# Sparse attention and a maxout layer on one Trainium2 core: the values of three batches in groups of 768 queries instead of 512

## The chip, the cores and the metric

The kernel runs on one core of a Trainium2 chip. Time is device time in microseconds (us) of one execution of the whole kernel. The core has a matrix engine (TensorE, PE in the profile), two engines that read and write the matrix engine's output memory PSUM (VectorE, DVE in the profile; ScalarE, ACT), a general engine[...] (GpSimd, POOL), and SyncE (SP), which here issues every load and store.

## The reference

Queries, keys and values have 4 batches, 8 heads, 768 positions and 64 columns per head. Each query sees the keys within 15 positions of its own and, beside them, 24 block summaries: the maximum of the keys over each block of 32, with the mean of the values there. The attention's result is the input of a maxout layer.

```python
k_sum = k.reshape(B, H, nb, block, D).max(axis=3)          # block 32, nb 24
v_sum = v.reshape(B, H, nb, block, D).mean(axis=3)
scores_l = where(|i - j| < 16, scale * q @ k.T, -1e9)
scores_s = scale * q @ k_sum.T + log(block)
a = softmax(concat([scores_l, scores_s]))
x = a @ concat([v, v_sum])                                 # then (B * S, H * D) = (3072, 512)
h1, h2 = x @ w1, x @ w2                                    # (512, 1024) each
out = maximum(h1, h2) @ w_out                              # (1024, 512)
```

## The kernel before

**Maxout.** `maximum(h1, h2)` is computed as `h1 + relu(x (w2 - w1))`. So the kernel makes `wd = w2 - w1` (four quarters, line 607), the product `w1 w_out` once (`make_w1o`, lines 636 to 650, matmuls on line 644), and then for each of 12 groups of 256 rows (`maxout`, line 652): eight columns of hidden units by `x wd` (line 660, "hidden"), a relu out of PSUM, and the output rows as `x (w1 w_out)` (line 674) plus `relu(...) w_out` (line 681), copied out of PSUM and stored. For `make_w1o` the quarters of w1 are cast to bf16 (`w1b`) and turned on TensorE (line 618, "turn w1"). The product runs over the 1024 hidden units in two halves: the first needs the first half of w1 and of w_out, the second the other halves. w1, w2 and w_out are each loaded in two halves of 1 MiB.

**Attention.** Heads are taken in pairs, four pairs a batch. Keys and queries of a pair are loaded, cast to bf16 (`casts`, on POOL, ACT or DVE), turned on TensorE (line 434), and placed in SBUF (`kx`, `qx`) together with the block maxima (line 454). The queries of a head pair are cut in three groups of 256 (`NG = 3`); a head pair and a group make a unit, named (hp, grp). `scores` (line 501) takes two units at a time: their scores fill two PSUM banks, ScalarE takes the exponent of all 1024 columns (line 515), and a product with a mask (line 509) hides what a query must not see. In batch 0 the mask is added by matmuls instead. The results `pb` have six buffers. Values come with a column of ones, so that the sum of the weights comes out as column 65 of each product.

**Values.** `values` (lines 523 to 555) takes the two units of one `pb`: 16 matmuls of 65 columns into two PSUM banks, one bank for each unit; one reciprocal of the eight sums (line 549); one multiplication of 2 x 4 x 64 columns with them (line 552), which writes `xs`. In batches 1 to 3 the pairs of units are (hp, 0) with (hp, 1), and (hp-1, 2) with (hp, 2): six calls a batch. In batch 0 they are the two head pairs of one group, six calls as well. `turn_x` (line 575) turns the rows of `xs` for the maxout layer, in batches 1 to 3 all three groups of two head pairs at once.

**PSUM** has eight banks. Scores, values and turns take two neighbouring ones, a hidden or output product one.

**What sets the order.** Nothing is decided when the kernel is built: the string `ORDER` lists every operation with its engine (P, A, D, G for POOL, S for SP), its number in the order of creation, and the buffer slots that it takes. `Plan.run` issues them in that order, so each engine has a fixed queue, SP's loads, stores and copies among them. An engine waits at the first operation of its queue whose inputs or slots are not free. In the text, "load v00" is the first half of batch 0's values, "load k01" the keys of batch 0, head pair 1, "hidden 001" the second quarter of batch 0, group 0.

The head of the kernel before on SP: eight k and q loads of batch 0, v00, v01, the first halves of w1 and w2, the first half of w_out, the second half of w1, of w_out and of w2; then batch 1. On TensorE: all turns of k and q of batch 0, the scores and values in between, then two hidden products (line 660), and then the run of `w1 w_out` products (line 644).

Of the kernel before, what the change touches and what calls it, by code (L numbers as in the profile page):

```python
# [12 lines left out]
F32 = mybir.dt.float32  # L13
BF16 = mybir.dt.bfloat16
AX = mybir.AxisListType
ALU = mybir.AluOpType
# [4 lines left out]
    "G5:0 D6:0 D1 D2 D0 S40:0,0 S36:1,0 S12:2,0 S39:3,0 G23:0,0,0 G4:0 S13:0 S37:0 A101:0 S38:0 G7 "  # L21
    "G32:0,0 P103:0,0 G8 S41:0 A105:1,0 G68:1 A77:2 S14:4 D106:0 G9 P70:2,0 G93:3 P79:4,0 S16:5 A72:2,0 "
    "D81:0,0 G10 P95:6,0 A69:0 S42:6 D108 D82:1 A78:1 P71:0 S43:7 D73:0 A76:0 P80:0 D3 D92:2 A85:1 D102:3 "
    "P94:0 A100:2 D83 P104:0 D107 D75 D84 A96:3,0 D74 S62:2 P90:2 D97:0 P86:4 A91:0 D15:0,0 A109:3 D98 "
    "P24:6 D18 D99 D19 P114:2 S52:1 A25 D21 A87:1 P88:0 D20 G22 P110:6 A89:2 P112:4 D17:0 S65:3 D26 A28 "
    "P33:0 D29 D27 A34 A113:3 D30 P116:0 D35 S53:0 A31 P126:4 A111:4 G45:0 D117:0 D127:1 D118:0,0 A49:1 "
    "D128:0 G48:0 P121:6 P46:0 D122:2 S147:4,0 D123:1,0 P50:4 A47:1,0 D51:0 P119:6 A120:0 P124:0 P136:4 "
    "D125 G63:0 A115:5 P131:6 P460:0 S146:0 D44:0 A64:0 D137:0 A461:0 P458:1 D138:0 G55:0 P455:2 A459 "
    "S153:5,0 D59:1 P56:3 P60:0 D57:0 P452:5 A61:0 D132:1 D67:0 P449:3 A66:0 D11:0 S150:2,0 D133:0 P446:4 "
    "P450 S152:0 P453 D58:0 S149:6,0 P456 A219:0 D54:0 S151:0 P447 A457:0 D218:1 S148:0 P129:0 P134:6 "  # L30
    "P462:2 G163:1,0,0,0 D130:1 A135 D454:0 S156:7 A448:0 P464:0 D463 A258:2 S154:3 P141:6 P221:4,0 "
    "A451:0 P220:0 P480:1 D257:3 A465 S171:0,0 D142:2 A222:0,0 P478:2 G231:0 D481:1 S173:1,0 P476:3 "
    "D226:0 A479 G246:1 P471:0 D223:1 P260:1,0 D224 P139:4 P259:0 D245:2 P472 A140:2 D143:0 G230:3 "
    "A261:2,0 S170:0 P482:4 D225 D265:1 A477 P484:5 A483 D262:0 P144:6 G157:0,0 P227:1 P247:3,0 A145 "
    "P248:0 P485 D249:1,0 A228:1 P232:6,0 S175:4,0 D263 P233:0 P473 A234:3,0 D229 S172:0 A253:2 P500:1 "
    "D251 D264 D236 D235:1 G155:0 A474:0 P486 A501:2 P496:2 A487:1 D237 S162 D238:3 G295:2 P164:3 S161 "
    "P494:4 G307:1 A165 D250:0 A168 A497 P489:0 G294:3 D166 A495 D167 P242:5 D158 S169 P239:1 P266:3 "
    "A243:2 P498:7 D159 A267:4 P490 D252 D244 P502:5 A499 D160 S178:5 A240:0 S180:2 P269:3 P254:6 D268 "
    "S174:0 P503 S196:6,0 D306:0 A270:3 P491 D241 A255:5 G187:0,0,0,0 P284:1 D271 P504 D285:0 A492:2 "
    "D286:2,0 P507:3 A505:3 S493 D256 P275:6 P272:0 P278:4 D276:1 P508 D273:2 G179:0,0 D279:0 D274:0,0 "  # L40
    "P466:2 D280:0 S177:7,0 D277:0 P287:0 P281:4 P467 D282:2 S195:3,0 D288:0 D283:0 P509 G181:0 D289:0 "
    "S199:0,0 P296:6,0 P297:0 D510:4 P290:4 S176:0 A298:0,0 P292:0 G322:3 D291:3 P468 A302:0 S186 G321:2 "
    "D293 P188:3 P308:4,0 G183 S198:0 P309:0 P324:6,0 A310:3,0 P323:0 D314:3 P518:0 S185 A329:1 D311:1 "
    "P514:1 A519:1 S182 P536:4 A469:5 S200:1,0 G382:0 A515 P512:5 S197:0 A325:2,0 P520:0 G333:1 A190 "
    "S194:0 D326:0 A189 P516:2 G334:3 A513 D313 P335:6,0 P336:0 D517 P530:1 A337:1,0 D537:2 A341:2 P521 "
    "D328 S184 D312 D327 D299:1 A371:2 P315:4 P330:6 P534:2 S201:0 A316:4 D339 D338:0 P522 S506 D192 D535 "
    "P532:4 A523:2 S470 D531 A331:0 P552:5 D300 D340 D301 P525:2 G383:1 D553:0 P303:0 D191 G370:3 P345:6 "
    "S193 P526 A304:1 D317 S202:5 P543:5 S204:2 G211:1,0,0,0 D533 A346:2 S475 D332 P318:0 P342:3 P544 "
    "A319:3 D305 P527 A343:5 D320 S488 P545 D528:3 P548:6 D546:5 P550:7 D344 A549 P357:0 A551 P354:3 S529 "
    "P351:5 D358:1 P538:2 D352:2 D355:0 D353:1,0 P554:7 D356:0 P561:5 D359:0,0 A555 P360:3 D347 P384:6,0 "  # L50
    "S524 P373:0,0 D361:2 G410:0 P372:0 P385:0 D362:0 P562 A374:2,0 S547 G409:2 D390:1 A378:0 P556:3 "
    "G205:0,0 D386:0,0 P563 P348:0 A564:0 G203:0 P363:6 P539 D349:0 D364:1 S565 D365:0 P557 D350:0 S207 "
    "G209 P412:4,0 S208 P411:0 P368:6 P366:0 S206 A369:0 P558 S511 D367 P540 G210 D387:0 A417:3 P586:0 "
    "D375:1 A398:3 P572:1 A587:1 D376 D397:1 P590:6 A559:1 D541:3 A413:3,0 P602:7 D377 D591 P212:0 A603:0 "
    "P584:3 D214 A215 D414:1 A573:2 P568:2 A585 D388 D416 P604:4 D389 A213 A216 S217 P570:5 A605 A569 "
    "P379:6 D571 P399:0,0 P391:3 A380:0 P400:0 P579:2 D401:1,0 A392:3 P588:5 D403 D381 P566:6 D402:1 A589 "
    "P597:7 A567 D405:2 P592:3 D415 D404 P574:4 P394:5 P421:0 P580 A395:4 P593 A422:5 P575 D423 P406:5 "
    "P418:0 D396 P581 A407:1 D393 P594 A582:2 D408 A419:2 P608:5 P576 A609 D420 A595:5 P598 A577:0 S596 "
    "P439:0 P433:5 S560 P424:2 D440:2 P599 D434:1 S578 D425:0 D426:2,0 P606:4 A600:4 D441:0,0 P615:2 "
    "D435:0 S601 A607 P436:0 P427:5 P430:3 D437:0 P610:7 D438:0 D431:2 P616 D428:1 D432:0 P611 D429:0 "  # L60
    "P444:0 P442:3 A445:3 P617 D443 P612 A618:5 P674:5 P624:6 P644:3 D625:2 P658:4 P620:0 P628:1 A621 "
    "A659:1 P656:2 P642:6 D657 P622:0 D613:1 D645:0 P626:4 S614 A623 D643 S583 P640:2 A627 P638:7 P629 "
    "D639 P669:3 D641 P664:0 P633:6 P660:4 P634 D661 P662:7 P630 D663 P651:2 A631:0 P635 P646:4 D636:4 "
    "P665 S637 S542 P647 S619 P652 S632 P648 P666 A649:1 P653 S650 A667:2 P675 S668 D654:4 P670 P676 S655 "
    "P671 A677:3 A672:5 S678 S673 "
# [81 lines left out]
def kernel(  # L147
# [50 lines left out]
    xsr = Ring(tiles("xs", 3, [128, NG, 2, 4, D], BF16))  # L198
# [324 lines left out]
    def values(b, units, pb, prio):  # L523

        ps, tag = Buf(banks, "av", 2), f"{b}" + "".join(f" {hp}{grp}" for hp, grp in units)
        pair = units[0][0] // 2
        if (b, pair) not in xs:
            xs[b, pair] = Buf(xsr)
        x, inv, part = xs[b, pair], Buf(invr), Buf(Ring([None]))
        for _, grp in units:  # L530
            x_part.setdefault((b, pair, grp), []).append(part)

        def av():
            return bank(ps, 1024).rearrange("p (c n) -> p c n", c=2)[:, :, 0:4 * (D + 1)].rearrange(
                "p c (j d) -> p c j d", j=4)

        def mm():
            for c, (hp, grp) in enumerate(units):
                for u in range(2):
                    for a in range(2):  # L540
                        for par in range(2):
                            at = 256 * c + 128 * u + 64 * par
                            nc.tensor.matmul(out=av()[64 * par:64 * par + 64, c, 2 * u + a, :],  # L543
                                             lhsT=pb.ap[:, a, at:at + 64],
                                             rhs=vx[b].ap[:, 4 * grp + 2 * u + par, 2 * hp + a, 0:D + 1],
                                             start=True, stop=True)

        op("PE", 0.235, mm, read=[pb, vx_part[b][pair]], touch=[vx[b]], write=[ps], prio=prio, label=f"values {tag}")
        op("DVE", 0.2, lambda: nc.vector.reciprocal(out=inv.ap[:], in_=av()[:, :, :, D:D + 1]),
           read=[ps], write=[inv], prio=prio, label=f"inv {tag}")  # L550
        (hp, grp), (_, g1) = units
        op("DVE", 0.69, lambda: nc.vector.tensor_tensor(  # L552
            out=x.ap[:, grp] if g1 == grp else x.ap[:, grp:g1 + 1, hp % 2], in0=av()[:, :, :, 0:D],
            in1=inv.ap[:].to_broadcast([128, 2, 4, D]), op=ALU.mult),
           read=[ps, inv], write=[x, part], prio=prio, label=f"x {tag}")
# [6 lines left out]
    def turn_x(b, pair, grps, prio):  # L562
# [7 lines left out]
        def mm():  # L570
            for n in range(4 * n_grp):
                for half in range(2):
# [3 lines left out]
                                        in_=x.ap[r, grps[n // 4], n // 2 % 2, i:i + 2].rearrange("p a d -> p (a d)"),  # L576
# [9 lines left out]
    invr = Ring(tiles("inv", 3, [128, 2, 4, 1], F32))  # L586
# [114 lines left out]
    def later_attention(b, base):  # L701
        pbs = []
        for hp in range(NP):
            prio = base + 20 * hp
            prep(b, hp, prio, {"DVE": 0.56, "POOL": 0.83}, {"ACT": 0.83, "POOL": 0.83})
            for units in ([(hp, 0), (hp, 1)], [(hp - 1, 2), (hp, 2)])[0:1 + hp % 2]:
                pbs.append((units, Buf(pbr)))
                scores(b, units, "DVE", pbs[-1][1], prio + 5)
        for units, pb in pbs:
            values(b, units, pb, base + 20 * units[-1][0] + 10)  # L710
# [3 lines left out]
    def first_attention():  # L714
# [8 lines left out]
        for grp in range(NG):  # L723
            for pair in range(2):
                prio = (20, 120, 220)[grp] + 2 * pair
                values(0, [(2 * pair, grp), (2 * pair + 1, grp)], pbs[pair, grp], prio)
# [55 lines left out]
```

## Time and profile before

| | us |
|---|---|
| median of 8 runs | 172.89 (172.4 to 173.75) |
| the profiled execution | 172.86 |
| its span in the trace | 171.1 |

The span runs from the first to the last instruction of the trace; 1.76 us of the execution lie around it. The largest groups of instructions, by line:

| line | what | instructions | busy us | mean ns |
|---|---|---|---|---|
| 660 | hidden products, 256 columns | 384 | 47.3 | 277 |
| 681 | relu times w_out | 200 | 46.4 | 371 |
| 674 | x times (w1 w_out) | 100 | 24.2 | 371 |
| 543 | values, 65 columns | 384 | 9.2 | 202 |
| 515 | exponents, ACT | 24 | 26.0 | 1113 |
| 549 | reciprocals, DVE | 24 | 4.4 | 198 |
| 552 | weighting of the values, DVE | 24 | 15.6 | 684 |

Matmuls overlap in the array, so a mean duration on TensorE is longer than the time from one to the next; what a group takes in a row is read from the chain of waits. "PEld" is the loading of the stationary operand, which runs beside the products. A line of the timeline gives start, duration, engine, source line, operation, output and input; in brackets stands how long the engine was idle before it and what ended that.

### The profile page before, as it was taken

The numbers are of one execution on the slowest core, as the hardware profiler recorded it, in microseconds if no ns is written. First come the engines' busy times: TensorE is split into PE (matmuls) and PEld (weight loads), VectorE is DVE, ScalarE is ACT, GpSimd is POOL, SyncE is SP. The second block draws the span as 40 slices with busy tenths as digits, with TensorE's granted clock in tenths as the row PEclk, the third lists the DMA queues.
The fourth block names the chain that finished last, engine by engine and source line by source line (L and its number), as shares of the span: only waits on it lengthen the run. The fifth ranks groups of instructions, "written<-read, shape, count | busy, mean of one in ns | idle before, by whom it ended". The sixth has DMA issues, their size and how long they took to land.

```text
span 171.1 us, 5208 instructions
## 1 busy us (share of the span) xinstructions
PE 152.3 (89%) x2256; PEld 98.9 (58%) x2256; DVE 106.1 (62%) x198; ACT 91.5 (53%) x128; POOL 42.5 (25%) x62
## 2 busy tenths in 40 slices
PE   0156866999999999997999999999999999999992
PEld 0034555655856755475765764787555658876451
DVE  1275998668788997867777696674543761443110
ACT  4488499646659695068658332778368231320121
POOL 7620135800355402496040029400000000000000
PEclk9999995699999999999999999999999999999999
DMA  5999899999999789999985995854000600030175
GB/s 181 300 341 220 208 399 385 387 379 371 295 211 299 238 168 220 314 384 231 280 256 101 238 287 205 186 122 83 8 0 15 234 4 0 4 123 0 49 258 184
DMA packets 43430, 34.92 MB, mean 204 GB/s; under 512 B 25968, under 2 KB 37392, under 8 KB 43408
## 3 DMA queue, kind: packets, MB, share of 16 engines
q1 hardware_dynamic: 43408, 34.61, 73.0%
q8 instruction: 17, 0.28, 0.7%
q14 instruction: 5, 0.04, 0.1%
HBM read 25.17 MB, written 6.29 MB: 184 GB/s over the span
## 4 chain that ended last, share of the span: by engine, by line
PE 83%; DMA 6%; ACT 4%; SPq 3%; issue 1%; DVE 1%; ACTq 0%
PE banks L660 26%; PE banks L681 25%; PE banks L674 12%; DMA land<-in_v_dram 6%; PE banks L543 4%; PE banks L501 4%; PE banks L644 4%; PE banks L434 3%; SPq L305 3%; ACT vx L410 2%; PE banks L575 2%; ACT pb L515 2%; PE banks L349 1%; PE banks L346 1%; PE banks L618 1%
## 5 line engine op out<-in xcount | busy, mean ns | idle before, releaser
L660 PE MATMUL banks<-xt,wd 128*128 128x256 bf16 x384 | 47.3, 277 | 0.9 <-issue 0.9
L681 PE MATMUL banks<-wo,g 128*128 128x512 bf16 (+1 forms) x200 | 46.4, 371 | 0.0
L660 PEld LDWEIGHTS <-wd 128*128 128x128 bf16 x384 | 37.4, 99 | 9.3 <-issue 1.1
L515 ACT ACTIVATE pb<-banks,bias 128x1024 bf16<-128x1024 f32 x24 | 26.0, 1113 | 6.4 <-PE banks L501 6.3
L681 PEld LDWEIGHTS <-g 128*128 128x128 bf16 x200 | 18.1, 98 | 17.2
L406 ACT ACTIVATE g<-banks 128x512 bf16<-128x512 f32 x30 | 17.6, 601 | 17.1 <-PE banks L660 17.0
L674 PE MATMUL banks<-w1o,xt 128*128 128x512 bf16 (+1 forms) x100 | 24.2, 371 | 0.0
L408 DVE TENSOR_SCALAR g<-banks 128x512 bf16<-128x512 f32 x18 | 12.1, 689 | 17.2 <-PE banks L660 16.4
L410 POOL CAST kqb<-land 128x768 bf16<-128x768 f32 x17 | 14.0, 835 | 31.0 <-PE banks L434 15.0
L410 ACT COPY o<-banks 128x512 f32<-128x512 f32 (+1 forms) x18 | 10.0, 564 | 20.4 <-PE banks L681 20.2
L434 PE MATMUL banks<-identity,kqb 64*128 64x64 bf16 x384 | 10.0, 202 | 10.4 <-ACT kqb L410 5.8
L454 DVE TENSOR_REDUCE ks<-kx 128x24 bf16<-128x768 bf16 x16 | 15.0, 945 | 6.2 <-ACT kx L410 6.2
L410 ACT COPY kx<-banks 128x768 bf16<-128x768 bf16 x12 | 9.7, 805 | 13.4 <-PE banks L434 13.4
L509 DVE TENSOR_TENSOR pb<-pb,mask 128x1024 bf16<-128x1024 bf16 x18 | 12.0, 687 | 6.6 <-ACT pb L515 6.6
L552 DVE TENSOR_TENSOR xs<-banks,inv 128x512 bf16<-128x512 f32 x24 | 15.6, 684 | 0.3
L434 PEld LDWEIGHTS <-kqb 64*128 64x128 bf16 x384 | 7.6, 102 | 13.5 <-ACT kqb L410 6.1
L674 PEld LDWEIGHTS <-xt 128*128 128x128 bf16 x100 | 9.5, 98 | 8.7
L410 POOL CAST vb<-land 128x1536 bf16<-128x1536 f32 x6 | 8.9, 1494 | 13.9 <-DVE pb L509 9.4
L543 PEld LDWEIGHTS <-pb 128*64 128x64 bf16 x384 | 7.8, 116 | 6.3 <-issue 4.2
L543 PE MATMUL banks<-vx,pb 128*64 128x65 bf16 x384 | 9.2, 202 | 2.5 <-ACT pb L515 1.8
L501 PEld LDWEIGHTS <-kx 64*128 64x128 bf16 x416 | 8.6, 103 | 4.6 <-issue 4.0
L410 ACT COPY xt<-banks 128x512 bf16<-128x512 bf16 (+1 forms) x6 | 5.2, 870 | 9.7 <-PE banks L575 9.7
(66 smaller groups left out, 146.3 us busy)
## 6 DMA issues: line engine op xcount, KB each, us to landing
land<-in_k_dram SPq DMA_DIRECT2D x16, 384.0 KB, 8.2
land<-in_q_dram SPq DMA_DIRECT2D x16, 384.0 KB, 7.6
land<-in_v_dram SPq DMA_DIRECT2D x8, 768.0 KB, 10.4
out_dram<-o SPq DMA_DIRECT2D x19, 256.0 KB, 2.6
land<-in_moe_w_dram SPq DMA_DIRECT2D x4, 1024.0 KB, 11.1
land<-in_moe_w_out_dram SPq DMA_DIRECT2D x2, 1024.0 KB, 12.9
vx<-vb SPq DMA_DIRECT2D x3, 396.0 KB, 6.5
vx<-vx SPq DMA_DIRECT2D x3, 363.0 KB, 4.1
```

The source lines that it names most:

```text
L406: nc.scalar.activation(out=o, in_=i, func=ACT.Relu)
L408: nc.vector.tensor_scalar_max(out=o, in0=i, scalar1=0.0)
L410: {"DVE": nc.vector.tensor_copy, "ACT": nc.scalar.copy, "POOL": nc.gpsimd.tensor_copy, "SP": nc.sync.dma_start}[e](out=o, in_=i)
L434: nc.tensor.transpose(out=bank(ps, 2048, BF16)[:, at:at + 64], in_=src.ap[r, j].rearrange("p h d -> p (h d)"), identity=identity[r, r])
L454: op("DVE", 0.95, lambda: nc.vector.tensor_reduce(out=ks.ap[:].rearrange("p (t s) -> p t s", s=2), in_=kt()[:, :, 0:64].rearrange("p t (s ...
L501: nc.tensor.matmul(**m)
L515: op("ACT", 1.13, lambda: nc.scalar.activation(out=pb.ap[:].rearrange("p a n -> p (a n)"), in_=bank(ps, 1024), func=ACT.Exp, bias=bias[:], ...
L543: nc.tensor.matmul(out=av()[64 * par:64 * par + 64, c, 2 * u + a, :], lhsT=pb.ap[:, a, at:at + 64], rhs=vx[b].ap[:, 4 * grp + 2 * u + par, ...
L552: op("DVE", 0.69, lambda: nc.vector.tensor_tensor(out=x.ap[:, grp] if g1 == grp else x.ap[:, grp:g1 + 1, hp % 2], in0=av()[:, :, :, 0:D], ...
L660: nc.tensor.matmul(out=bank(ps)[:, 256 * s:256 * s + 256], lhsT=wd[n].ap[:, c, 128 * s:128 * s + 128], rhs=x_rows(b, grp)[:, c, :], start= ...
L674: nc.tensor.matmul(out=bank(ps, hi - lo), lhsT=x_rows(b, grp)[:, c, sl], rhs=w1o[c].ap[:, lo:hi], start=(c == 0), stop=False)
L681: nc.tensor.matmul(out=bank(ps, hi - lo), lhsT=g.ap[:, f, sl], rhs=wo[f // 2].ap[:, f % 2, lo:hi], start=False, stop=(f == FC - 1))
```

## The change

In batches 1 to 3 `values` takes the three units of one head pair, (hp, 0), (hp, 1) and (hp, 2), which lie in two different `pb` buffers, the third one shared with the neighbouring head pair. Their 24 matmuls fill the same two PSUM banks, six products of 65 columns in each, and one reciprocal of 12 sums and one multiplication of 2 x 6 x 64 columns serve all three: four calls a batch instead of six. Batch 0 keeps two units a call. `xs` is laid out with the head pair ahead of the group, so that the multiplication writes 768 columns in a row, and `turn_x` reads it by the new addresses.

```diff
-    xsr = Ring(tiles("xs", 3, [128, NG, 2, 4, D], BF16))
+    xsr = Ring(tiles("xs", 3, [128, 2, 4 * NG, D], BF16))
...
-    def values(b, units, pb, prio):
+    def values(b, units, pbs, prio):
...
+        n_unit = len(units)
+        per = 2 * n_unit
...
-            return bank(ps, 1024).rearrange("p (c n) -> p c n", c=2)[:, :, 0:4 * (D + 1)].rearrange(
-                "p c (j d) -> p c j d", j=4)
+            return bank(ps, 1024).rearrange("p (c n) -> p c n", c=2)[:, :, 0:per * (D + 1)].rearrange(
+                "p c (j d) -> p c j d", j=per)
...
-            for c, (hp, grp) in enumerate(units):
+            for n, (hp, grp) in enumerate(units):
+                pb, c = pbs[n]
...
-                            at = 256 * c + 128 * u + 64 * par
-                            nc.tensor.matmul(out=av()[64 * par:64 * par + 64, c, 2 * u + a, :],
+                            at, j = 256 * c + 128 * u + 64 * par, 4 * n + 2 * u + a
+                            nc.tensor.matmul(out=av()[64 * par:64 * par + 64, j // per, j % per, :],
...
-        op("DVE", 0.69, lambda: nc.vector.tensor_tensor(
-            out=x.ap[:, grp] if g1 == grp else x.ap[:, grp:g1 + 1, hp % 2], in0=av()[:, :, :, 0:D],
-            in1=inv.ap[:].to_broadcast([128, 2, 4, D]), op=ALU.mult),
+        op("DVE", 0.13 + 0.275 * n_unit, lambda: nc.vector.tensor_tensor(
+            out=x.ap[:, :, 4 * grp:4 * grp + 4] if g1 == grp else x.ap[:, hp % 2].rearrange(
+                "p (c j) d -> p c j d", c=2), in0=av()[:, :, :, 0:D],
+            in1=inv_ap().to_broadcast([128, 2, per, D]), op=ALU.mult),
...
-        for units, pb in pbs:
-            values(b, units, pb, base + 20 * units[-1][0] + 10)
+        for hp in range(NP):
+            units = [(hp, grp) for grp in range(NG)]
+            values(b, units, [pb_of[unit] for unit in units], base + 20 * (hp | 1) + 10)
```

The list of operations is shorter by 18 (three for each call less), and `ORDER` is written anew from its first word to its last: every engine's queue differs, and some casts, copies and relus stand on another engine. The head of it on SP is now: k of head pairs 1, 0 and 3, v00, q of 0, 1 and 3, v01, k and q of head pair 2, then the first half of w1, the first half of w_out, the second half of w1, the second half of w_out, the first and the second half of w2; then batch 1. On TensorE the first hidden product stands behind all eight `w1 w_out` products of line 644:

```diff
-    "P24:6 D18 D99 D19 P114:2 S52:1 A25 D21 A87:1 P88:0 D20 G22 P110:6 A89:2 P112:4 D17:0 S65:3 D26 A28 "
-    "P33:0 D29 D27 A34 A113:3 D30 P116:0 D35 S53:0 A31 P126:4 A111:4 G45:0 D117:0 D127:1 D118:0,0 A49:1 "
...
+    "P80:0 D74 D20 A85:1 D26 A102:1 P88:6 S62:7 D108 D19 P86:2 A89:0 P90:0 S52:3 P104:0 A87:1 D17:0 S65:1 "
+    "A91:2 D109:2 P33:6 G92:2 D30 P126:2 A34 G29 P116:4 A93:3 D127:0 P136:0 S43:0 D128:0,0 P94:6,0 D137:1 "
...
```

## The prediction

> **What bounds the kernel now.** I read the page's shares first, then the chain of waits, then the windows of the first 36 us, the transfers of the first 45 us, and the timeline where these pointed. The shares and the chain:
>
> ```profile
> PE 152.3 (89%) x2256; PEld 98.9 (58%) x2256; DVE 106.1 (62%) x198; ACT 91.5 (53%) x128; POOL 42.5 (25%) x62
> PE 83%; DMA 6%; ACT 4%; SPq 3%; issue 1%; DVE 1%; ACTq 0%
> ```
>
> TensorE carries the end. The span is 171.1 us, so it idles 18.8 us. By the windows of 5 us it is busy 15.15 of the first 30 us, so 14.85 us of the idle lies there; the rest is one stall of 0.88 us at 78 us with no releaser, and about 3 us behind the last matmul (168.0). VectorE is busy 62% and nearly off the chain: work taken from it is worth nothing by itself. What can move the end is (1) when TensorE's unbroken stretch starts, (2) how long its work takes after that, (3) a new stall in it. For (2), the chain in order of time shows a fixed price:
>
> ```profile
> 62.69 0.62 PE banks L501 x36
> 63.31 1.83 PE banks L681 x8
> 65.14 0.38 PE banks L543 x16
> 65.52 0.97 PE banks L681 x4
> 66.48 0.86 PE banks L674 x4
> 67.35 0.89 PE banks L543 x48
> ```
>
> Four 512-column matmuls take 0.86 us in stream and 0.97 behind small packed matmuls; 16 value matmuls take 0.38 alone and 48 take 0.89, that is 0.25 per 16 plus 0.12 once. So each separate run of small matmuls between large ones costs 0.11 + 0.12 = 0.23 us, whatever is in it.
>
> For (1), the windows (columns: stretch, busy time by engine, granted clock, DMA share, GB/s) and the transfers of the first 45 us in slices of 1.125 us:
>
> ```profile
> 18.00:19.00 1.00, 1.00 (x6) 0.46 (x4) 0.97 (x3) 0.00 (x0) 0.54 (x1) 1.00 0.39 69
> 19.00:20.00 1.00, 1.00 (x27) 0.78 (x28) 0.97 (x3) 0.81 (x2) 0.00 (x0) 1.00 0.51 75
> 27.00:28.00 1.00, 1.00 (x40) 0.94 (x38) 0.92 (x3) 0.68 (x1) 1.00 (x1) 0.50 1.04 385
> 32.00:33.00 1.00, 1.00 (x7) 0.72 (x6) 0.30 (x2) 0.60 (x1) 0.23 (x2) 0.55 1.05 385
> ...
> GB/s 0 52 339 341 205 291 382 366 391 384 282 221 206 220 233 220 65 148 404 410 391 390 399 380 388 390 380 388 390 395 377 385 376 371 371 376 374 373 371 317
> ```
>
> Loads run without a break from 2 to 45 us, at 385 GB/s but for the two v loads (about 220), with one hole at 18 to 20 us where the last v load ends and the first weight load starts: 69 and 75 GB/s over 2 us are 144 KB, which v's rate of 220 moves in 0.65 us, so about 1.4 us stand unused. The granted clock is one half from 26 to 33 us. The timeline then says what the loads hold up:
>
> ```profile
> 23.16 1.30 POOL L410 CAST w1b<-land 128x1024 bf16<-128x1024 f32 x1 [4.62 <-DMA land<-in_moe_w_dram]
> 25.92 2.35 POOL L607 TENSOR_TENSOR wd<-land,land 128x1024 bf16<-128x1024 f32 x1 [1.46 <-DMA land<-in_moe_w_dram]
> 30.02 2.04 POOL L410 CAST wo<-land 128x1024 bf16<-128x1024 f32 x1 [1.75 <-DMA land<-in_moe_w_out_dram]
> 32.70 0.69 DVE L410 CAST w1b<-land 128x1024 bf16<-128x1024 f32 x1 [0.70 <-DMA land<-in_moe_w_dram]
> 38.10 2.36 DVE L607 TENSOR_TENSOR wd<-land,land 128x1024 bf16<-128x1024 f32 x2 [1.02 <-DMA land<-in_moe_w_dram]
> ```
>
> These waits date the six weight loads: the 1st is in at 23.1, the 2nd at 25.9, the 3rd at 30.0, the 4th at 32.7, the 6th at 38.1; the 5th (w_out's second half) before its cast at 35.6. TensorE is unbroken from 34.35 us, when it gets the weights of the 4th load.
>
> **What the Trainium skill says.** "TensorE: Matmul & The Clock Gate", Part 1: the clock is half at the start and after an idle window of about 3.4 us, full after a busy one, and the windows run on their own phase. The trace agrees: half from 26.1 to 32.9, twice 3.4 us, behind a window with few matmuls. Its record says 1.00 before the first change, but six 256-column matmuls took 1.46 us at 17.7 and 0.84 at 22.6, so the start was slow too. "DMA: Bandwidth & Descriptors", Specifications: under 512 B a transfer is off line rate; v's rows of 256 B are the ones seen at 220 GB/s. "PSUM — Partial Sum Buffer", Specifications: a bank holds 512 FP32 values, so 6 x 65 = 390 columns fit where 4 x 65 = 260 stood; no wait comes from the size.
>
> **The change part by part.** *Values.* Batches 1 to 3 go from 18 groups of 16 matmuls, 18 reciprocals and 18 weightings to 12 of 24, 12 and 12. The matmuls are the same 288. VectorE: six reciprocals of 0.198 us go, 1.2 us. A weighting of 512 took 0.684 and a PSUM copy of 128 columns 0.289, so 1.03 ns a column and 0.95 us for 768: 12 x 0.95 = 11.4 against 18 x 0.684 = 12.3. Together 2.1 us less VectorE, hidden behind TensorE: 0 on the path. A pair's values now wait for its third unit's exponent; in the new order all three stand several large groups ahead, so I charge nothing; were that cover gone, one exponent and mask is 1.11 + 0.69 us a time. Order of parts in xs and the turned rows' addresses: same counts, nothing.
>
> *Order.* All queues are rewritten, and this is what counts. On TensorE, runs of small matmuls behind the first hidden product fall from 29 to 22.
>
> *Head.* On SP, v00 is now 4th, v01 8th, and the six weight loads go w1a, w_out a, w1b, w_out b, w2a, w2b instead of w1a, w2a, w_out a, w1b, w_out b, w2b (a and b are halves). The ten k, q and v loads ahead of them are the same bytes, so I keep the six dates by position. Then:
> - w1a at 23.1; POOL's two casts of it, 1.35 each: 25.8. The turn of w1 0 at half clock (1.04, the row of before at 27.4): 26.9. Three scores with mask at the cadence of 0.85 seen at 20 to 22 us: 29.5. The first half of w_out is in between 25.9 (2nd place) and 28 (lag of the 3rd), its cast on POOL 2.04: 29.9 at worst. So the first product w1·w_out starts near 30.0.
> - Four such halves 3.5, two turns 0.9 and a switch 0.2: 34.6; two values 0.6: 35.2. The second halves need w_out b, in at 32.7, and two VectorE casts of 0.65: 34.0, in time. Four halves 3.5, values and two turns 0.5, three switches 0.4: the first hidden product at 39.6.
> - It needs w2a, now 5th: 35.4, and POOL's subtraction 2.35: 37.8. Slack 1.8. The last needs w2b at 38.1 and VectorE (subtraction 1.2, a relu 0.7, a cast 0.55, subtraction 1.2 in turn): 43, against 39.6 + 5 x 0.87 + 0.1 = 44. Slack 1.
>
> At 39.6 the kernel before stands in its w1·w_out run, which ends at 41.14. So at that moment the changed one is ahead by 1.54 of it, one values group (0.25) and three turns of x (0.36), and behind by two hidden products (2 x 0.87): 0.4 us. From there it has 22 packed runs against 28: 6 x 0.23 = 1.4. Sum 1.8 us.
>
> *Two corrections.* Holes behind v loads: before has one of 1.4 us; after has two, v00 to q and v01 to k. The only v-to-q edge in this trace, at 51 us, shows one second at 168 GB/s, so 0.55 us. Two of those are 1.1, 0.3 better; bounds 0 and 2 x 1.4, so from 1.4 better to 1.4 worse. Clock: TensorE is dense from 25.8, so the first whole dense window ends between 29.2 and 32.6 by the phase; what lies behind 30.0 runs the products at half speed and loses half of it, 0 to 1.3 us, 0.5 in the mean; 1.7 if one more gap spoils that window. Before lost nothing lasting, since the 4th load held it until 34.35.
>
> 172.86 - 1.8 - 0.3 + 0.5 = 171.3 us. The 172.86 is the profiled execution (span 171.1 and 1.76 around it); the median shown is 172.89, so the two frames agree. The tail is kept at 3 us: the last group still ends in two half copies and stores.
>
> *In the dense part.* One spot is tight: near 105 us the copy of an output on ScalarE needs a buffer that a store frees, and SP has that store behind the spread of the means, two k loads and two v loads. Before, from that spread's issue at 90.4 the v loads ended at about 100.8 and the next store by 102: some 11.5 us. Two k loads and one store more make 14.2, with the copy 15; my count of TensorE's groups between the means and the turn that needs the bank gives 17 to 18. Covered by 2 us; priced at 0 with an end of 2 for the range.
>
> **The rivals.**
> - *Forecast (0.55):* earlier products and fewer packed runs, 171.3; own range 169.9 to 172.3.
> - *More (0.10):* no holes and a full clock from 30 us: 172.86 - 1.8 - 1.4 = 169.7. For it: SP has the loads queued well ahead. Against it: the one v edge that I can see is not free.
> - *Even (0.14):* the clock stays half through the first products (1.7): 172.8. For it: the phase is free and the head has idle windows. Against it: turns and scores fill 25.8 to 30.
> - *Slower (0.21):* v is cut in two in the queue, and each cut leaves a hole like the one at 18 to 20 us. All weight loads are then 1.4 us late, the products start 1.4 later, and the late start leaves 1.7 at half clock: 172.86 - 1.8 + 1.4 + 1.7 = 174.2. It decides from 1.8 us of delay on. For it: TensorE has no other work in the new order, since both hidden products that bridged 30 to 33 us now stand behind the products with w_out.
> - That the change does not do what it says can be left out: the new order has 12 values groups for three batches.
>
> **The numbers.** About 0.3% (0.5 us) is what a measurement tells from no change. Forecast and more give faster but for a few hundredths: 0.63. Even, and the upper edge of the forecast: 0.15. Slower 0.22. The range takes the forecast's, most of "more" and the lower part of "slower", where one hole is 1.4 and the clock costs 1: 169.4 to 173.8.
>
> **What would show it.** Right: 18 weightings, 6 of 0.68 and 12 near 0.95 us; the first hidden product at 38.5 to 40.5; TensorE unbroken from about 30; chain pieces of 0.97 rarer. Wrong: w2a's subtraction later than 39 us; TensorE's end not earlier than 166.7 though the first hidden product came by 39.6 (then stalls in the dense part, to be looked for at 105 us); small runs that cost less than 0.23.

## The result, and the profile after

| | us | runs | ratio to before, 95% interval |
|---|---|---|---|
| before | 172.86 median (172.03 to 173.75) | 32 | |
| changed kernel | 170.62 median (168.26 to 172.18) | 11 | 0.983, 0.980 to 0.986 |
| changed kernel, measured again | 170.03 median (169.51 to 171.14) | 6 | 0.9816, 0.978 to 0.985 |

By the medians the kernel became faster by 2.2 to 2.9 us, by the ratios by 2.9 to 3.2; the prediction was 171.3, 1.6 us less than before. The medians are of all runs, the ratios here and below only of those within 1.5% of a kernel's fastest (six of the eleven in the first row of the changed kernel), and its first profiled execution, 171.99 us, lies above that band, so the lines below are from the second one: 171.14 us, span 169.4. That too is 1.1 us above its median, so the trace shows less of the gain than the runs do.

The page's shares and the chain of waits, where the page of before had 152.3 us of TensorE and 83% of the chain on it:

```profile
PE 150.2 (89%) x2256; PEld 97.4 (58%) x2256; DVE 108.8 (64%) x187; ACT 91.2 (54%) x125; POOL 41.7 (25%) x66
PE 64%; SPq 15%; DMA 7%; DVE 6%; issue 3%; ACT 2%; POOL 1%; DVEq 0%; ACTq 0%; POOLq 0%
```

TensorE's busy time fell by 2.1 us with the same 2256 matmuls (by 0.8 in the first profile). The chain now leaves TensorE twice in the dense part, by VectorE and by SP's queue with a store: two waits are new there, and both are taken up below. VectorE has eleven instructions less and yet 2.7 us more: two copies of 3.17 us stand on it that before didn't have there.

The values in the chain in order of time (start, length):

```profile
126.85 0.86 PE banks L681 x4
127.71 0.88 PE banks L546 x48
128.59 0.97 PE banks L688 x4
```

The weightings in the groups by form (busy time, mean ns, idle before):

```profile
L557 DVE TENSOR_TENSOR xs<-banks,inv 128x768 bf16<-128x768 f32 x12 | 11.1, 953 | 0.2
L557 DVE TENSOR_TENSOR xs<-banks,inv 128x512 bf16<-128x512 f32 x6 | 3.9, 684 | 0.1
```

Twelve weightings have 768 columns, and batch 0's six keep 512. 48 value matmuls are now two groups of three units and take the same 0.88 us as three groups of two did (0.89). The price at the edges is the same, 0.97 against 0.86.

The head, first in four windows of 1 us (engines' busy time, clock, DMA share, GB/s):

```profile
18.00:19.00 1.00, 0.92 (x6) 0.65 (x6) 0.99 (x2) 1.00 (x2) 0.73 (x1) 1.00 1.06 386
19.00:20.00 1.00, 1.00 (x35) 0.62 (x35) 0.58 (x2) 0.68 (x3) 0.94 (x2) 1.00 1.10 397
27.00:28.00 1.00, 1.00 (x23) 0.64 (x18) 0.99 (x2) 1.00 (x2) 0.00 (x0) 0.50 1.04 385
32.00:33.00 1.00, 1.00 (x22) 0.46 (x22) 0.84 (x2) 0.00 (x1) 0.00 (x0) 1.00 1.09 393
```

The transfers of the first 45 us, in slices of 1.125 us:

```profile
GB/s 0 29 253 381 360 284 230 226 306 370 361 263 218 225 303 373 378 400 382 386 382 386 395 379 391 382 391 390 382 388 377 377 373 371 378 359 284 246 207 116
```

And the timeline of the same stretch, with what waits for the weight loads:

```profile
22.99 2.10 POOL L409 CAST w1b<-land 128x1024 bf16<-128x1024 f32 x2 [1.70 <-DMA land<-in_moe_w_dram]
25.61 1.05 ACT L409 CAST wo<-land 128x1024 bf16<-128x1024 f32 x1
25.64 1.04 POOL L409 CAST wo<-land 128x1024 bf16<-128x1024 f32 x1 [0.54 <-DMA land<-in_moe_w_out_dram]
27.40 2.97 PE L651 MATMUL banks<-wo,vx 128*128 128x512 bf16 x8
28.35 1.29 DVE L409 CAST w1b<-land 128x1024 bf16<-128x1024 f32 x2 [0.20 <-DMA land<-in_moe_w_dram]
33.74 2.35 POOL L614 TENSOR_TENSOR wd<-land,land 128x1024 bf16<-128x1024 f32 x1 [7.07 <-DMA land<-in_moe_w_dram]
37.83 5.41 PE L667 MATMUL banks<-xt,wd 128*128 128x256 bf16 x48
```

The hole of before at 18 to 20 us (69 and 75 GB/s) is gone: 386 and 397, and neither of the two v loads of 220 GB/s leaves one behind it. The first half of w_out is cast as soon as it is in, its two quarters at once on POOL and ScalarE, so the first product with w_out starts at 27.4 instead of 33.4 us. Its eight matmuls take 2.97 us, since the clock is at first still half (0.50 in the window of 27 to 28 us). The first hidden product stands at 37.8 (38.6 in the first profile), and from there 48 hidden matmuls run in one piece.

In the dense part, three lines of the timeline of the first profiled execution:

```profile
60.56 3.17 DVE L409 COPY vx<-vx 32x5808 bf16<-32x5808 bf16 x1
68.33 1.02 PE L681 MATMUL banks<-w1o,xt 128*128 128x512 bf16 x4 [1.61 <-DVE g L407]
106.07 0.86 PE L581 MATMUL banks<-identity,xs 64*128 64x64 bf16 x47 [0.54 <-ACT o L409]
```

The timeline of the second at the same places:

```profile
62.95 1.89 DVE L508 TENSOR_TENSOR pb<-pb,mask 128x1024 bf16<-128x1024 bf16 x3
64.75 1.47 POOL L409 CAST vb<-land 128x1536 bf16<-128x1536 f32 x1 [8.12 <-DMA land<-in_v_dram]
65.49 1.28 DVE L508 TENSOR_TENSOR pb<-pb,mask 128x1024 bf16<-128x1024 bf16 x1
68.82 0.52 PE L581 MATMUL banks<-identity,xs 64*128 64x64 bf16 x23 [0.17 <-DVE xs L557]
70.51 0.20 PE L581 MATMUL banks<-identity,xs 64*128 64x64 bf16 x1 [1.17 <-issue]
105.23 0.86 PE L581 MATMUL banks<-identity,xs 64*128 64x64 bf16 x47 [0.54 <-ACT o L409]
```

From 59 to 71 us VectorE has hardly any free time (busy 11.7 of 12 us): the spread of batch 1's means (3.17 us in both executions, in before a DMA of SP), four masks, a relu, four weightings. Where masks fall beside a cast on POOL, one takes 1.28 us instead of 0.63, and TensorE waited 1.61 us for the relu behind them in the first execution, 0.17 us in the second. The wait at 105 us is the same in both: ScalarE's copy of an output needs a buffer that a store frees. The 1.17 us with no releaser is of the kind of the 0.88 us of before at 78 us; the first execution has none (see the end).

### The profile page after: what moved, and what is told of

Same layout as the page of the kernel before. It is cut to its first block, busy times and chain, and to the rows that moved or that the text cites. A ratio compares the mean times of both kernels' runs of the same rounds, so it can differ in the third digit from the quotient of the medians.

```text
span 170.3 us, 5181 instructions
## 1 busy us (share of the span) xinstructions
PE 151.5 (89%) x2256; PEld 98.6 (58%) x2256; DVE 110.0 (65%) x187; ACT 91.1 (54%) x125; POOL 42.9 (25%) x66
## 4 chain that ended last, share of the span: by engine, by line
PE 65%; SPq 15%; DMA 8%; DVE 5%; issue 2%; ACT 2%; POOL 1%; DVEq 0%; ACTq 0%; POOLq 0%
PE banks L667 22%; PE banks L688 19%; PE banks L681 9%; SPq L304 8%; PE banks L651 5%; DMA land<-in_moe_w_dram 5%; PE banks L500 4%; SPq L326 4%; SPq L699 3%; DMA out_dram<-o 3%; PE banks L433 2%; PE banks L546 2%; DVE vx L409 2%; DVE pb L508 2%; PE banks L581 2%
## 5 line engine op out<-in xcount | busy, mean ns | idle before, releaser
L667 PE MATMUL banks<-xt,wd 128*128 128x256 bf16 x384 | 45.7, 273 | 0.0
L409 POOL CAST kqb<-land 128x768 bf16<-128x768 f32 x21 | 19.2, 934 | 43.7 <-PE banks L433 21.1
L405 ACT ACTIVATE g<-banks 128x512 bf16<-128x512 f32 x34 | 20.0, 605 | 18.6 <-PE banks L667 15.2
L514 ACT ACTIVATE pb<-banks,bias 128x1024 bf16<-128x1024 f32 x24 | 25.6, 1113 | 5.8 <-PE banks L500 5.7
L409 ACT COPY o<-banks 128x512 f32<-128x512 f32 (+1 forms) x15 | 8.6, 570 | 19.8 <-PE banks L688 10.8
L508 DVE TENSOR_TENSOR pb<-pb,mask 128x1024 bf16<-128x1024 bf16 x18 | 13.9, 796 | 5.8 <-ACT pb L514 5.7
L407 DVE TENSOR_SCALAR g<-banks 128x512 bf16<-128x512 f32 x14 | 9.6, 687 | 11.3 <-PE banks L667 11.2
L409 ACT COPY xt<-banks 128x512 bf16<-128x512 bf16 (+1 forms) x7 | 6.6, 955 | 17.0 <-PE banks L581 13.1
L557 DVE TENSOR_TENSOR xs<-banks,inv 128x768 bf16<-128x768 f32 (+1 forms) x18 | 15.0, 862 | 0.3
L409 DVE COPY o<-banks 128x512 f32<-128x512 f32 (+1 forms) x10 | 6.6, 662 | 13.0 <-PE banks L688 13.0
L409 POOL CAST vb<-land 128x1536 bf16<-128x1536 f32 x6 | 8.8, 1467 | 11.7 <-PE banks L500 7.4
L500 PE MATMUL banks<-qx,kx 64*128 64x64 bf16 (+2 forms) x416 | 10.2, 199 | 0.9 <-ACT qx L409 0.9
```

Of the source, the lines that this page charges most:

```text
L405: nc.scalar.activation(out=o, in_=i, func=ACT.Relu)
L409: {"DVE": nc.vector.tensor_copy, "ACT": nc.scalar.copy, "POOL": nc.gpsimd.tensor_copy, "SP": nc.sync.dma_start}[e](out=o, in_=i)
L500: nc.tensor.matmul(**m)
L508: nc.vector.tensor_tensor(out=o, in0=o, in1=m, op=ALU.mult)
L514: op("ACT", 1.13, lambda: nc.scalar.activation(out=pb.ap[:].rearrange("p a n -> p (a n)"), in_=bank(ps, 1024), func=ACT.Exp, bias=bias[:], ...
L557: op("DVE", 0.13 + 0.275 * n_unit, lambda: nc.vector.tensor_tensor(out=x.ap[:, :, 4 * grp:4 * grp + 4] if g1 == grp else x.ap[:, hp % 2].r ...
```

## The experiments

"Before" in each is the kernel before, measured beside it on the same chip. Diffs of the order are given in the names of the operations.

**1. Only the wide values, in the order of before.** Each three-unit group stands where the later of its two-unit groups stood; 27 packed runs instead of 28.

```diff
-  PE: values 1 00 01 | ... | values 1 02 12        (18 groups in batches 1 to 3)
+  PE: values 1 00 01 02                             (12 groups)
```

> The three-unit values alone, in the order of the kernel before: each wide group stands where the later of its two narrow groups stood. Theory (the gain of the change is its new order: earlier products, fewer packed runs): VectorE does about 2 us less, but hidden behind TensorE; 27 packed runs behind the w1 w_out products against 28, so 0.2 us less; 172.3 to 173.3 us, with the kernel before at 172.9. Rival (the gain is the shorter VectorE work and the shared weighting): close to the changed kernel, 170.3 to 171.3 us.

Measured: 173.62 us, before 173.13; ratio 1.0034 (1.0015 to 1.0052). The order of the head is as before; the values alone gain nothing, and this is even a little slower. The code part of the change, taken by itself, isn't the gain.

**2. Only the new order, with the narrow values.**

```diff
-  PE: values 1 10 11 12 | values 1 00 01 02 | (2 large) | values 1 30 31 32 | values 1 20 21 22 | ...
+  PE: values 1 10 11    | values 1 00 01    | (2 large) | values 1 02 12 | values 1 30 31 | values 1 20 21 | ...
```

The third units of two head pairs follow as one group in the next run of small matmuls (`values 1 22 32` one run further on).

> The code of before (18 narrow values groups for batches 1 to 3) in the order of the changed kernel: each three-unit group is replaced by its two-unit group at its place, and the pair's third units follow as a narrow group in the next run of small matmuls, so that the packed runs are 23 as in the changed kernel; VectorE does 2.1 us more. Theory (the order alone gains, the wide values nothing): 170.3 to 171.3 where before stands at 173.0, ratio 0.985 to 0.990, not distinguishable from the changed kernel. Rival (the three-unit values are needed for the gain, by VectorE or by PSUM coming free sooner): 172.0 to 173.0, ratio 0.994 to 1.000.

Measured: 175.79 us, before 172.88; ratio 1.0147 (1.0099 to 1.0195). Both expectations missed: it is 5.8 us slower than the changed kernel measured beside it (170.03). Its timeline shows seven waits of TensorE for VectorE, 5.3 us together, where the changed kernel's second profile has 0.17 us and its first 1.61; four of them:

```profile
67.76 1.02 PE L672 MATMUL banks<-w1o,xt 128*128 128x512 bf16 x4 [1.23 <-DVE g L406]
103.95 0.44 PE L541 MATMUL banks<-vx,pb 128*64 128x65 bf16 x16 [0.77 <-DVE xs L550]
108.50 0.53 PE L432 MATMUL banks<-identity,kqb 64*128 64x64 bf16 x24 [1.03 <-DVE xs L550]
139.45 0.41 PE L573 MATMUL banks<-identity,xs 64*128 64x64 bf16 x16 [0.78 <-DVE xs L550]
```

The first is for a relu, at the place where the changed kernel's first profile waits too. In the other six, values and turns wait for a weighting (`xs`), which holds their banks or their rows. The new order leaves two large groups between values and their next user; with the third units a run later, that is too short. So the order, as it stands, needs the wide values, though they gain nothing without it. Other places for the third units weren't tried.

**3. The price of a packed run.** The changed kernel with ten more runs: a large group is moved between two small ones. The first of these places is at 93 us, most lie behind 100; one of them:

```diff
-  PE: turn q33 | turn k32 | hidden 221
+  PE: turn q33 | hidden 221 | turn k32
```

> The changed kernel with ten large groups of TensorE moved forward by one place, each from behind a pair of small groups to between the two, all behind 100 us: the same matmuls, ten more runs of small ones. Theory (each separate run costs 0.23 us): 2.3 us more, 172.5 to 173.5 against 170.6. Rival (the 0.97 against 0.86 in the chain is only how the ends of overlapping matmuls are modelled): 170.6 within 0.5.

Measured: 173.32 us, before 173.23; ratio 0.9983 (0.9957 to 1.001). Against the changed kernel's 170.62 that is 2.7 us for ten, 0.27 each, with intervals of about 0.5 us on either side. The traces are sharper: from the scores at 93 us, just ahead of the first moved group, to the last matmul TensorE takes 75.27 us here. In the changed kernel's second profile it is 73.57 with the 0.54 of waiting at 105 us, which this run doesn't have, and 72.91 in the profile of experiment 8 with the stores early, which hasn't either. That is 2.2 to 2.4 us for ten, the 0.23 each that was read from the chain; so these are no matter of how the ends of matmuls are modelled.

**4. The new load order undone.** The changed kernel with the first half of w2 loaded second, as in before.

```diff
-  SP: w1a, w_out a, w1b, w_out b, w2a, w2b
+  SP: w1a, w2a, w_out a, w1b, w_out b, w2b
```

> The changed kernel with w2's first half loaded second again, as before, so that the first half of w_out comes third and everything behind it one place later. Theory (the place of the loads sets when the products start): the first product starts 2 to 3 us later than its 28.2, and all behind it; 172.3 to 173.6 us against 170.6. Rival (TensorE has slack there, since it waits for the 5th load anyway): 170.6 within 0.5.

Measured: 174.06 us, before 173.13; ratio 1.0039 (1.0017 to 1.0062); 3.4 us slower than the changed kernel, more than expected. TensorE stands before the first products and before the turns of w1:

```profile
31.16 1.89 PE L649 MATMUL banks<-wo,vx 128*128 128x512 bf16 x7 [1.18 <-POOL wo L407]
34.02 0.41 PE L623 MATMUL banks<-identity,w1b 64*128 64x64 bf16 x16 [0.98 <-DVE w1b L407]
```

The first hidden product stands at 41.9 us. One megabyte earlier in SP's queue costs more than the whole change gains: in the new order nothing else is there for TensorE to do between 29 and 34 us.

**5. The new load order alone, in the kernel before.** The two early hidden products go behind the products with w_out.

```diff
-  SP: w1a, w2a, w_out a, w1b, w_out b, w2b
+  SP: w1a, w_out a, w1b, w_out b, w2a, w2b
-  PE: hidden 001 | hidden 000 | w1o (8 groups)
+  PE: w1o (8 groups) | hidden 001 | hidden 000
```

> The kernel before with nothing but its head changed: loads in the order w1a, w_out a, w1b, w_out b, w2a, w2b, and the two hidden products of 001 and 000, with their subtractions and relus, behind the w1 w_out products. Theory (the head is about half of the gain): the products start 3 to 5 us earlier than 34.35 in the trace, the first hidden product comes near 39, and the time falls by 0.5 to 1.5 us, to 171.4 to 172.4. Rival (the head is hidden by what follows, or the wide values are the gain): 172.9 within 0.3.

Measured: 174.17 us, before 173.13; ratio 1.0061 (1.0042 to 1.008). Missed: a loss instead of about 1 us gained.

```profile
31.00 1.01 PE L642 MATMUL banks<-wo,vx 128*128 128x512 bf16 x2 [0.32 <-ACT wo L408]
41.14 0.19 PE L573 MATMUL banks<-identity,xs 64*128 64x64 bf16 x1 [0.41 <-ACT g L404]
```

The load comes earlier, but the second quarter's cast stands on ScalarE behind exponents, and behind the early products nothing fills TensorE; when the hidden products come, the turns behind them wait for relus. In this form, without the casts and the filling work, the load order is worth nothing.

**6. The whole head of the changed kernel, in front of the order of before.** Every queue up to the first hidden product is the new one (39 groups on TensorE, 22 loads), with narrow values and 28 packed runs behind it.

```diff
-  PE: ... turn w1 0 | turn w1 1 | turn x000 | ... | hidden 001 | hidden 000 | w1o ...
+  PE: ... turn w1 0 | scores 0 20 30 | scores 0 21 31 | scores 0 22 32 | w1o ... | hidden 001 | hidden 000
```

> The kernel before with the changed kernel's whole head (all queues up to the last w1·w_out product, 39 groups on TensorE, with its load order and its casts), and the order of before behind it; narrow values, 28 packed runs behind the last w1·w_out product as before. Theory (the new head brings about 1.3 us when it is taken whole, the fewer packed runs the rest): 171.2 to 172.2 us where before stands at 173.0, ratio 0.990 to 0.996; first hidden product at 38.4 to 38.9. Rival (the head brings nothing, as the moved loads alone did, and the gain is all in the later order): 172.6 to 173.4, ratio 0.998 to 1.002.

Measured: 173.17 us, before 172.88; ratio 1.0026 (1.0003 to 1.0049). The first hidden product comes at 38.6 as expected, but the time is the rival's:

```profile
38.61 1.92 PE L658 MATMUL banks<-xt,wd 128*128 128x256 bf16 x16
42.91 1.03 PE L658 MATMUL banks<-xt,wd 128*128 128x256 bf16 x8 [1.03 <-ACT xt L408]
```

At 42.9 the join between the two orders loses 1.03 us: a hidden product waits for a copy of turned rows that ScalarE has behind two relus and two casts. So that one was moved:

```diff
-  ACT: relu 001 | relu 000 | cast q10 | w1o 3 | xt 011
+  ACT: xt 011 | relu 001 | relu 000 | cast q10 | w1o 3
```

> The kernel with the changed kernel's head and the order of before behind it, with one instruction moved: ScalarE's copy of the last turned x of the head stands ahead of the first relu instead of behind two relus and two casts, where its hidden product waited 1.03 us for it. Theory (the whole head is worth about 1.1 us, and the join to the old order had eaten it): 171.8 to 172.5 us where before stands at 173.0, ratio 0.993 to 0.998. Rival (the head brings nothing lasting; the next wait takes the place of this one): 172.8 to 173.5, ratio 0.999 to 1.003.

Measured: 173.52 us, before 173.16; ratio 1.0036 (1.0014 to 1.0057). Missed again, and the reason is in the trace:

```profile
27.84 1.90 PE L642 MATMUL banks<-wo,vx 128*128 128x512 bf16 x8
37.26 1.92 PE L658 MATMUL banks<-xt,wd 128*128 128x256 bf16 x16
43.80 0.83 ACT L408 CAST kqb<-land 128x768 bf16<-128x768 f32 x1 [1.82 <-POOL kqb L408]
45.17 1.91 PE L658 MATMUL banks<-xt,wd 128*128 128x256 bf16 x16 [2.12 <-ACT w1o L408]
```

The hidden products now start at 37.3, earlier than in any other profile, and the wait of 1.03 us is gone. In its place TensorE waits 2.12 us for a copy of `w1o` out of its bank. That copy stands on ScalarE behind the cast of q13, and q13 is the seventh of batch 1's loads in the new load order where it was the third in the old one. The cast starts at 43.8 us here and at 43.9 in the run before, however early TensorE is. The trace of the run before has ScalarE waiting 1.01 us for the load of q there, the one here for a cast of POOL; so it is the loads, or a cast behind them, that date it. The changed kernel has six hidden products in one piece at this place (48 matmuls, 37.83 to 43.2 us), just until batch 1's turns are ready. The start that the head gains is kept by what stands behind it. What the head alone is worth, free of a join, these runs don't tell.

**7. VectorE's time.** The changed kernel with the reciprocal and the weighting of three units cut in two, one for each bank.

```diff
-  inv: reciprocal 2 x 6          x: multiply 2 x 6 x 64
+  inv: 2 reciprocals of 6        x: 2 multiplications of 6 x 64
```

> The changed kernel with the wide reciprocal and the wide weighting of batches 1 to 3 cut in two, one for each PSUM bank: 12 more reciprocals of 0.2 us and 12 more weightings, 4.3 us more VectorE work in all. Theory (VectorE is off the path but for the stretch at 58 to 70 us): 170.5 to 171.6 us against 170.6. Rival (the sharing is what makes the kernel faster): 172.5 us or more.

Measured: 171.13 us, ratio 0.9879 (0.9847 to 0.9911); 0.5 us above the changed kernel by the medians, 0.8 to 1.1 by the ratios, whose intervals just overlap.

```profile
L564 DVE TENSOR_TENSOR xs<-banks,inv 128x384 bf16<-128x384 f32 x24 | 11.7, 541 | 0.0
L558 DVE RECIPROCAL inv<-banks 128x6 f32<-128x6 f32 x24 | 3.1, 171 | 2.9 <-PE banks L546 2.9
```

The two groups take 11.7 and 3.1 us here, 11.1 and 2.2 in the changed kernel's second profile. So VectorE has not 4.3 but 1.5 us more, since neighbouring instructions overlap: as much as the wide values save in experiment 1 (104.6 us busy against 106.1 in before). Taking that saving back costs at most 1.1 of the 5.8 us of experiment 2. VectorE's total isn't what the wide values bring; by exclusion, and by the waits shown there, most of that difference is where the third units stand.

**8. The two waits of the dense part.** First the relu of 67 us two masks earlier on VectorE; then five entries of SP (two stores, three loads) ahead of the spread of batch 2's means, for the wait at 105 us; then both.

```diff
-  DVE: mask 1 30 31 | mask 1 22 32 | relu 020 | mask 1 20 21
+  DVE: relu 020 | mask 1 30 31 | mask 1 22 32 | mask 1 20 21
...
-  SP: spread means 2 | load k33 | load v31 | load v30 | store 021 | ... | store 000
+  SP: store 021 | store 000 | load k33 | load v31 | load v30 | spread means 2
```

> The changed kernel with one relu (batch 0, group 2, first quarter) two masks earlier on VectorE. TensorE waited 1.6 us for it at 67 us, behind the spread of the means (3.17 us on VectorE) and three masks. Theory (that wait is a real loss of the new order): 0.8 to 1.6 us less, 169.0 to 169.8. Rival (what waits next takes its place, masks and weightings being as late): 170.6 within 0.4.

> The changed kernel with five entries of SP's queue (the stores of 021 and 000, the keys of batch 3, pair 3, and both v loads of batch 3) ahead of the spread of batch 2's means, which waits for its input until 88.7 us while the transfers are idle. Theory (the 0.5 us that TensorE waits at 105 us for an output buffer goes, nothing else does): 170.0 to 170.5. Rival (the spread now stands behind v in the queue and batch 2's values wait for it): 171 or more.

> The two edits of the relu and of the five entries of SP together. If both waits are losses of their own: 1.3 to 2.1 us less than the changed kernel, 168.5 to 169.3. If what is behind them takes their place: 170.6 within 0.5.

Measured: 171.05 (ratio 0.9894, 0.9845 to 0.9942), 170.37 (0.9811, 0.9764 to 0.9858) and 170.25 us (0.9826, 0.9791 to 0.986). None differs from the changed kernel beyond the intervals. With the relu early, the second group of values waits instead:

```profile
63.90 3.79 DVE L506 TENSOR_TENSOR pb<-pb,mask 128x1024 bf16<-128x1024 bf16 x3
65.86 2.51 POOL L407 CAST kqb<-land 128x768 bf16<-128x768 f32 x2
68.87 0.57 PE L544 MATMUL banks<-vx,pb 128*64 128x65 bf16 x24 [1.00 <-DVE xs L555]
```

Three masks take 3.79 us beside POOL's casts, and the values miss the banks that the weightings free. The next wait has taken the place of the one removed, as the rival had it. With the stores early no wait is left at 105 us, but the profile with only the early relu has none there either, and experiment 7's has 1.06 us. So this place is tight as well, and what the stores' edit is worth these runs don't tell: 0.54 us is less than the intervals are wide.

**9. The changed kernel once more,** without an edit, for the second profile.

> The changed kernel once more, for a second profile. Theory (the 1.6-us wait at 67 us belongs to one execution, in which three masks ran beside POOL's casts): median 170.2 to 171.2, the first hidden product again at 38.4 to 38.9, no wait over 0.5 us on TensorE near 67 us. Rival (the wait is part of the order): the same wait of 1 to 2 us at 66 to 69 us, and masks of 1.2 us each there.

Measured: 170.03 us, ratio 0.9816 (0.9782 to 0.9851), first hidden product at 37.83; both lie a little below what was expected. Near 67 us 0.17 us of waiting is left of 1.61, with masks of 0.63: in this execution POOL's cast of v, which waited 8.1 us for its load, came 1.8 us behind the start of the masks, in the first one 0.6 us. In the other profiles of this order TensorE waits for VectorE there for 0 (experiments 7 and 8, stores early) to 1.3 us (both versions with the early relu), so the place is tight, and how much it costs goes with the time at which POOL's casts fall.

## Why the prediction was right, and where it wasn't

**The bound and the price of a run: right.** 0.23 us for each separate run of small matmuls was read from the chain; ten added runs cost 0.22 to 0.24 each in the traces of experiment 3. "TensorEngine Tiling (Array Packing)" of the Trainium skill, Key Properties, says that a change of tiling mode drains TensorE, without a figure. That this drain is what a run costs fits the trace, but no run here separates it from other causes. Behind the first hidden product the changed kernel has 22 runs, where before has 28 from the end of its products with w_out on, so 1.4 us, as predicted.

**Weighting and VectorE: right in size, too simple in place.** 12 weightings of 0.953 us (0.95 predicted), 6 of 0.684; VectorE's busy time fell by 1.5 us in experiment 1, where 2.1 was summed. That this saving is worth nothing by itself was borne out (experiment 1). "I charge nothing" for the later third units held because the new order leaves room; experiment 2 shows what it costs where that room is gone, 5.3 us of waits.

**The head: the mechanism right, its terms too long.** Predicted were the first product with w_out at 30.0, the first hidden product at 39.6 and 0.4 us ahead there; seen were 28.2 and 27.4, 38.6 and 37.8. By the prediction's own sum (the rest of before's w_out run to 41.14, plus 0.25 and 0.36, less 1.74) that is 1.4 us ahead in the first profile and 2.2 in the second. The prediction had 0.4, and 0.2 with its corrections for holes and clock. The second profile's 37.8 also lies ahead of the 38.5 to 40.5 that it had named as a sign of being right.
- The cast of w_out, "29.9 at worst", didn't hold anything up: the load was in at 25.6 and the two quarters were cast on two engines at once, done at 26.7.
- TensorE's own path to the first product, summed to 29.5, was too long as well. POOL's two casts of w1 took 2.10 us where 2.7 was charged, and the turn of one quarter of w1 took 0.25 us (0.42 in the first profile) where 1.04 was charged. That 1.04 is a misreading, since the row of before holds the turns of two quarters:

```profile
27.39 1.04 PE L618 MATMUL banks<-identity,w1b 64*128 64x64 bf16 x32
25.15 0.41 PE L625 MATMUL banks<-identity,w1b 64*128 64x64 bf16 x16 [0.54 <-POOL w1b L409]
```

  The first line is from before, the second from the changed kernel, where the scores follow at 25.40 us. They took 2.0 us (2.7 in the first profile, 2.6 predicted), and the products started at once behind them.
- The correction for holes behind v loads, two of 0.55, was too careful: there is none. (The microsecond at 51 us in before, from which it was taken, moved 186 GB/s and not 168, which changes the 0.55 by 0.03.) The rival that had them at 1.4 us each, the slower one, fails at its first step, 386 and 397 GB/s at 18 to 20 us.
- The clock cost what was allowed for: eight products 2.97 us instead of 1.83, so 1.1 of the 0 to 1.3 us. Where the half-clock stretch ends differs from one execution to the next; "TensorE: Matmul & The Clock Gate", Part 1, says that its windows run freely and don't start with the kernel. In the ten profiles with this head the full clock is back between 27.3 and 30.5 us. Where it is back by 28.3, the first hidden product stands at 37.3 to 38.0; where it comes behind 30.1, at 38.5 to 38.7. The two runs of experiment 6, with the same head, have it back at 30.4 and at 27.3, and differ by 1.35 us at the first hidden product.

**The dense part: the step that was wrong.** It was priced at no loss, with one tight spot at 105 us "covered by 2 us". It wasn't covered: both profiles wait 0.54 us there.

```profile
87.86 0.60 SPq L409 DMA_DIRECT2D vx<-vx  x1
104.59 0.59 ACT L409 COPY o<-banks 128x512 f32<-128x512 f32 x1 [2.15 <-DMA out_dram<-o]
```

From the issue of the spread to the copy that the store releases are 16.7 us in both profiles, where 14.2 was summed; and TensorE was there after 16.8, where 17 to 18 was counted. And the prediction missed 59 to 71 us, where VectorE is full. It costed VectorE by its total over the kernel, and gave no price to the spread of the means, which moved to it: one copy of 3.17 us in front of four masks. "SBUF — State Buffer" of the skill, Who interferes with whom, says that a VectorE instruction with two SBUF inputs contends with a GpSimd one that reads SBUF; a mask is of that kind, and it takes 0.63 us alone and 1.27 beside a cast. The move could be seen in the order, and the masks' place behind it; its length could not, since before had such a copy only at half the length (0.97 us, so an estimate of 1.9).

So two errors offset each other, and that the number came out so near is luck. For the second profile: 2.2 ahead at the first hidden product, 1.4 for the runs, less 0.17 and 0.54 of new waits and 0.29 by which the gap without a releaser is longer, gives 2.6; TensorE's end moved by 1.8, from 168.0 to 166.2. The first profile gives 1.4 + 1.4 - 1.3 = 1.5 (waits of 1.61 and 0.54, and no gap without a releaser) against 1.0 seen. About 0.7 and 0.5 us aren't placed by this sum. Either way the whole lead is there at the first hidden product, and the dense part, which was forecast to add 1.4 us to it, took 0.4 us away in both profiles. The check that the prediction had named (an end later than 166.7 though hidden products came by 39.6 means stalls in the dense part) was met by the first profile, at 167.0.

**What the experiments add.** The prediction summed a head and fewer runs as if each stood alone. They don't: the wide values in the old order give +0.3%, the new order with narrow values +1.5%, the new load order in the old kernel +0.6%, the whole new head in front of the old order +0.3%. Together they give -1.7 to -1.8%. Each piece moves a wait to a place where nothing is ready; in the whole, what is lost at such places is less than what is gained.

## What to carry to other kernels

When a rewritten order gains, don't look for the one edit that did it before asking what stands behind it: a start that comes 1 us earlier is kept only if the next loads, casts and copies were moved as well, and it is worth finding the first thing that is dated by a transfer. In pricing such a change, list each operation that changes its engine, and add it to that engine's busiest stretch, not to its total. And count the runs of small matmuls between large ones: their number has a price of its own, about a quarter of a microsecond each here.

## What the runs showed of the hardware

- A copy of 32 partitions x 5808 bf16 columns on VectorE takes 3.17 us in each profile of the new order, also where POOL stands still beside it; one of half that length took 0.97 us in before. Why the long one is not twice the short one wasn't tried.
- VectorE and POOL lengthen each other: three masks take 1.89 us alone and 3.79 beside POOL's casts, and these casts 1.77 and 1.25 us where 1.47 and 0.80 were usual (early relu).
- In eight of the fourteen profiles TensorE stands still once without a releaser, and at a fixed place in its instructions: for 0.9 to 1.25 us ahead of the 1120th matmul in all five kernels that have the dense part in the order of before, and for 1.0 to 1.3 us ahead of the 992nd in three of the nine with the new order, so 128 matmuls earlier. So two single profiles can differ by about 1 us through this alone. The packed traces hold one more hint: the page of each profile has a queue named "instruction",

```profile
q8 instruction: 17, 0.28, 0.7%
```

  and in all fourteen this matmul starts 1.4 us or more behind the landing of the last of that queue's 16-KB packets. In the eight that stand still it is 1.4 to 1.7 us. That looks like a wait of TensorE for its own instructions; no experiment moved it, so it isn't shown.
